# Logits beside the gate/up remainders, four units to a group, the last output in two PSUM tiles and a later output projection

## The chip, the cores and the metric

One core of a Trainium2 chip runs the whole program. The metric is the device time of one execution in microseconds (us); the kernel before took 577.35 us (median of 6 runs, 576.67 to 954.04; the highest is one run, left out of all ratios). The granted TensorE clock was 0.999 of full speed in the profiled execution.

The engines are called PE (TensorE, matmuls; PEld is its weight load), ACT (ScalarE), DVE (VectorE), POOL (GpSimd) and SP (SyncE); ACTq is ACT's queue of transfers. PSUM, in banks, is the memory that PE writes its results to.

## The reference, cut to what matters

A block with adaptive layer norm: attention over 8 dilated neighbours (32 heads of 18), then a bilinear gated MLP. There are 2048 tokens of width D = 576, and F = 4608 hidden units.

```python
h = layernorm(x) * (1 + ca) + sa
q, k, v = split(h @ wqkv)                      # 32 heads of 18
logits[s, w] = q[s] . k[s - 2 w], w = 0..7     # masked at the start
x = x + ga * (softmax(logits * scale) @ v[neighbours]) @ wo
h = layernorm(x) * (1 + cb) + sb
x = x + gb * ((h @ w_gate) * (h @ w_up)) @ w_down
```

## The kernel before: the parts that matter

The 2048 tokens go through attention in ten chunks (four of 128 tokens, six of 256). Gate/up runs in seven passes: four of 128 tokens, then three of 512. After every 512 tokens comes a "down" (four row blocks of 36 x 2 matmuls). While PE works on one pass, the attention of the next chunks is woven into its order by a pacer, a function that the kernel calls after every few matmuls: a table gives, for each piece of attention, the fraction of the period at which it is put in.

```python
AT = dict(lg0=.06, lg1=.14, lgT=.19, hT=.31, ...)                # fractions of a period
AT_FIRST = dict(AT, ..., oT=.66, wo0=.70, wo1=.74, h2T=.92)      # chunks 4 and 5 use this one
...
ps_att = pool("ps_att", 2, space=PSUM)      # 2 banks, attention
ps_mlp = pool("ps_mlp", 3, space=PSUM)      # 3 tiles of 2 banks, MLP
v_sb = once.tile([P, D], BF, name="v_sb")   # one buffer for v on its way to DRAM
```

The width of 576 is four blocks of 128 and a remainder of 64. Gate and up share the array for the remainder: gate's uses rows 0 to 63, up's rows 64 to 127, and the two matmuls run side by side in a tiling of 64 x 128. To save changes of tiling, three units (a unit is gate and up of 128 hidden columns for 512 tokens) form a group:

```python
for u in range(0, len(units), 3):
    for k in range(3):
        ps[u + k] = ps_mlp.tile([P, 2, nf, 512 // nf], F32, name="pgu", tag="mlp")
        if k < 2:
            main(u + k, True)            # 8 plain matmuls; then step(): the pacer may put in attention
    for k in range(3):
        rem(u + k, k == 2)               # 2 remainder matmuls each, 64*128 tiling
    step(6 * nf * ns / 2)
    evacuate(u); evacuate(u + 1)         # ACT copies PSUM out, DVE multiplies gate by up
    main(u + 2, False); evacuate(u + 2)
    ...                                  # cut: what follows a finished block
```

The logits of attention are also small matmuls: 20 of them in a 128 x 32 tiling, called `lgT`. A chunk has two such groups (pieces `lg0` and `lg1`).

The last row block of the whole output is done in two halves of 288 columns, so that the first half can be stored early. Both halves lie in one PSUM tile:

```python
for j in range(CM // P):
    acc = ps_mlp.tile([P, 2, 512], F32, name="acc", tag="mlp")
    halves = [[0], [1]] if r0 + (j + 1) * P == S else [[0, 1]]
    for qs in halves:
        ...                              # 36 or 72 matmuls into acc[:, q], then DVE reads acc and stores
```

In the attention of a chunk, `turn` transposes the attention output on PE into PSUM, ACT copies it to `oT` (two copies), and `wo0`, `wo1` are the output projections of the two 128-row halves. The v of a half goes from PSUM through `v_sb` (two ACT copies) to DRAM.

Of the kernel before, what the change touches and what calls it, by code (L numbers as in the profile page):

```python
# [8 lines left out]
F32 = mybir.dt.float32  # L9
# [8 lines left out]
P = 128  # L18
D = 576
DP = 640  # L20
KT = 5
# [11 lines left out]
CH = 256  # L33
# [3 lines left out]
FB = 4  # L37
AUTO = 4
GU_BUFS = 3
NB = FT // FB  # L40
# [14 lines left out]
AT = dict(lg0=.06, lg1=.14, lgT=.19, hT=.31, q0=.37, q1=.41, k0=.45, k1=.49, qkr=.52, v0=.55, v1=.58,  # L55
          ws=.60, oT=.61, wo0=.66, wo1=.70, h2T=.86)

AT_FIRST = dict(AT, hT=.24, q0=.29, q1=.34, k0=.39, k1=.44, qkr=.48, v0=.52, v1=.57, ws=.64, oT=.66, wo0=.70, wo1=.74, h2T=.92)

AT_SHORT = dict(AT_FIRST, qkr=.47, ws=.51, oT=.52, wo0=.59, v0=.66, v1=.72, h2T=.80)  # L60


@with_exitstack
def kernel(
# [13 lines left out]
    nc = tc.nc  # L78
# [7 lines left out]
    def pool(name, bufs, **kw):  # L86
        return ctx.enter_context(tc.tile_pool(name=name, bufs=bufs, **kw))
# [13 lines left out]
    ps_mlp = pool("ps_mlp", 3, space=PSUM)  # L101

    def att(shape, dt, name):
        return ps_att.tile(shape, dt, name=name, tag="att")

    def hp():
        return tc.high_priority()
# [11 lines left out]
    for sl, m0, off in ((slice(0, KT), 0, 0), (slice(KT, KT + 1), KT - 1, -64)):  # L119
        n = sl.stop - sl.start  # L120
# [15 lines left out]
    hT = once.tile([P, KT, CH], BF, name="hT")  # L136
# [5 lines left out]
    oT = once.tile([P, KT, CH], BF, name="oT")  # L142
# [7 lines left out]
    def load_x(ci, eng, js=None, behind=None):  # L150

        for j in range(SIZES[ci] // P) if js is None else js:
            xt = xin.tile([P, D], BF, name="x_t")
            if behind is not None:
                nc.vector.tensor_copy(xt[0:1, 0:1], behind)
            eng.dma_start(xt[:], x_flat[START[ci] + j * P:START[ci] + (j + 1) * P, :])
            x_tiles.setdefault(ci, []).append(xt)
# [16 lines left out]
    v0 = sp.tile([P, D], BF, name="v0")  # L174
# [83 lines left out]
    rows = {}  # L258
# [20 lines left out]
    gu_blocks = {}  # L279
# [53 lines left out]
    def block_done(pi, b):  # L333
        if pi == KEPT_PASSES - 1 and b in KEPT:
            k = KEPT.index(b)
            load_wd(k * WDB, (k + 1) * WDB)
        for n in range(len(loads)):
            if last_use[n] == (pi, b) and n + GU_BUFS == state["next"]:
                load_next(eng=nc.gpsimd if pi == 0 else nc.sync)
        if (pi, b) == (0, ORDER[0][-2]):  # L340

            for cx in (4, 5):
                load_x(cx, nc.sync, behind=late["hh"][0:1, b * FB, 0:1])
            f0 = len(KEPT) * WDB
            nc.vector.tensor_copy(wd[0:1, f0, 0:1], late["hh"][0:1, b * FB, 0:1])
            load_wd(f0, FT)
# [301 lines left out]
    def gate_up(pi, c0, C, h2, step):  # L648




        hh = late["hh"]
        cs = slice(c0, c0 + C)
        ns = C / 2.4

        def tokens(rows, kt):
            return h2[rows, :, kt, :] if C > CH else h2[rows, c0 // CH, kt, c0 % CH:c0 % CH + C]

        def by_half(ap):  # L660
            return ap.rearrange("p (a c) -> p a c", c=CH) if C > CH else ap


        nf = 2 if C <= 256 else 1
        units = [(b, i) for b in ORDER[pi] for i in range(0, FB, nf)]

        def main(u, first):
            (b, i), out = units[u], ps[u]
            for n in range(nf):
                for t in range(2):  # L670
                    for kt in range(KT - 1):
                        nc.tensor.matmul(by_half(out[:, t, n, 0:C]), lhsT=gu_blocks[b][0][:, kt, t, (i + n) * P:(i + n + 1) * P], rhs=tokens(slice(0, P), kt),  # L672
                                         start=(first and n == 0 and kt == 0), stop=(not first and kt == KT - 2), skip_group_check=True)
                step(8 * ns)

        def rem(u, first):
            (b, i), out = units[u], ps[u]
            for n in range(nf):
                for t in range(2):
                    rows = slice(64 * t, 64 * (t + 1))  # L680
                    nc.tensor.matmul(by_half(out[:, t, n, 0:C]), lhsT=gu_blocks[b][1][rows, (i + n) * P:(i + n + 1) * P], rhs=tokens(rows, KT - 1),  # L681
                                     start=(first and n == 0), stop=not first, skip_group_check=True)

        def evacuate(u):
            b, i = units[u]
            fs = slice(b * FB + i, b * FB + i + nf)
            with hp():
                g = late["gup"].tile([P, 2 * CM], BF, name="gu")[:, 0:2 * nf * C].rearrange("p (n t c) -> p n t c", n=nf, t=2)
                nc.scalar.copy(g, ps[u][:, :, :, 0:C].rearrange("p t n c -> p n t c"))  # L689
                nc.vector.tensor_tensor(hh[:, fs, cs], g[:, :, 0, :], g[:, :, 1, :], ALU.mult)  # L690


        ps, done = {}, 0
        for u in range(0, len(units), 3):
            for k in range(3):
                ps[u + k] = ps_mlp.tile([P, 2, nf, 512 // nf], F32, name="pgu", tag="mlp")
                if k < 2:
                    main(u + k, True)
            for k in range(3):
                rem(u + k, k == 2)  # L700
            step(6 * nf * ns / 2)
            evacuate(u)
            evacuate(u + 1)
            main(u + 2, False)
            evacuate(u + 2)
            while done < NB and (done + 1) * FB <= (u + 3) * nf:
                block_done(pi, ORDER[pi][done])
                done += 1

    def down(di, r0, x_t, step):  # L710
        to_load = [(cx, j) for cx in LOAD_X_DOWN.get(di, []) for j in range(SIZES[cx] // P)]
        hh = late["hh"]
        for j in range(CM // P):
            acc = ps_mlp.tile([P, 2, 512], F32, name="acc", tag="mlp")

            halves = [[0], [1]] if r0 + (j + 1) * P == S else [[0, 1]]
            for qs in halves:
                for f in range(FT):
                    for q in qs:
                        nc.tensor.matmul(acc[:, q, 0:288], lhsT=hh[:, f, j * P:(j + 1) * P], rhs=wd[:, f, q * 288:(q + 1) * 288],  # L720
                                         start=(f == 0), stop=(f == FT - 1))
                    step(120 * len(qs))
                with hp():
                    n, cs = len(qs), slice(qs[0] * 288, (qs[-1] + 1) * 288)
                    o_t = outp.tile([P, D], BF, name="y")[:, 0:n * 288]
                    nc.vector.tensor_tensor(o_t.rearrange("p (n d) -> p n d", n=n), acc[:, qs[0]:qs[-1] + 1, 0:288],  # L726
                                            gb_bc[:, cs].rearrange("p (n d) -> p n d", n=n), ALU.mult)
                    nc.vector.tensor_tensor(o_t, o_t, x_t[j][:, cs], ALU.add)  # L728
                (nc.gpsimd if n == 2 else nc.sync).dma_start(out_flat[r0 + j * P:r0 + (j + 1) * P, cs], o_t)  # L729
            if to_load:  # L730
                cx, jx = to_load.pop(0)
                load_x(cx, nc.gpsimd, [jx])

    h2T = {}
    home = {c: (di, START[c] - START[d[0][0]]) for di, d in enumerate(DOWN) for p in d for c in p}

    def attend_into_place(ci):
        di, c0 = home[ci]
        if di not in h2T:
            h2T[di] = h2p.tile([P, CM // CH, KT, CH], BF, name="h2T")  # L740
        return attend(ci, h2T[di][:, c0 // CH, :, c0 % CH:c0 % CH + SIZES[ci]])

    def period(ci):

        gens = {"a": project(ci + 1)} if ci + 1 < NCH else {}
        gens["b"] = attend_into_place(ci)
        at = AT_SHORT if SIZES[ci] == P else AT_FIRST if ci < 6 else AT
        nxt = {k: next(g) for k, g in gens.items()}
        while nxt:
# [3 lines left out]
            if nxt[k] is None:  # L753
                del nxt[k]

    class Pacer:


        def __init__(self, todo, total):
            self.todo, self.L, self.t, self.i, self.gen, self.nxt = todo, total / max(1, len(todo)), 0.0, 0, None, None  # L760

        def __call__(self, ns, rest=False):
            self.t += ns
            while self.i < len(self.todo):
                if self.gen is None:
                    if self.t < self.i * self.L and not rest:
                        return
                    self.gen = period(self.todo[self.i])
                    self.nxt = next(self.gen)
                if self.t < (self.i + self.nxt) * self.L and not rest:  # L770
                    return
                self.nxt = next(self.gen, None)
                if self.nxt is None:
                    self.gen, self.i = None, self.i + 1
                elif not rest:
                    return
# [49 lines left out]
    passes = [(di, p) for di, d in enumerate(DOWN) for p in d]  # L826
# [49 lines left out]
```

## Time and profile before

| | before |
|---|---|
| median time, us | 577.35 |
| span of the profiled execution, us | 576.4 |
| PE busy | 562.7 us (98%) |
| DVE, ACT, POOL busy | 55%, 38%, 17% |
| chain that ended last, PE's share | 84% |

The first lines of the page, busy time by engine:

```profile
PE 562.7 (98%) x5167; PEld 369.0 (64%) x5171; DVE 318.0 (55%) x695; ACT 221.5 (38%) x386; POOL 95.7 (17%) x165
```

PE is the bound, so a gain must come from time in which PE does its fixed work badly ordered, or waits. The view of waits for PE shows few waits; these three touch the change (in us: total, times, longest):

```profile
PE acc L720 <- ACT gu L689: 0.6, 1, 0.6
PE pwA L628 <- ACT oT L621: 0.6, 1, 0.6
PE acc L720 <- DVE y L726: 0.5, 1, 0.5
```

The chain that ended last, in order of time, is the best view for a bound engine: consecutive pieces add up to the span. Its columns are start, duration, and what, with the number of matmuls. First, a stretch of the first 512-token pass:

```profile
208.95 3.45 PE pgu L672 x16
212.40 0.78 PE lgT L553 x20
213.19 0.76 PE pgu L681 x6
213.94 3.56 PE pgu L672 x16
217.50 0.78 PE lgT L553 x20
218.28 1.83 PE pgu L672 x8
220.12 0.75 PE pgu L681 x6
220.87 1.83 PE pgu L672 x8
```

L672 are the plain matmuls, L681 the remainders, L553 the logits. Sixteen plain matmuls take 3.45 us (0.216 each) when they follow plain ones, but 3.56 after remainders; eight take 1.83 instead of 1.73 after remainders or after logits. Leaving a tiling mode costs 0.105 us. Six remainders are three pairs, 3 x 0.216 = 0.65, and take 0.755: entering costs 0.107. The first logits group of the chunk stands directly before remainders; the second (217.50) stands between plain matmuls and so pays an exit of its own.

The last pass, the same view: groups of 6 remainders and 24 plain matmuls, a change in and a change out every 6.04 us.

```profile
497.70 0.76 PE pgu L681 x6
498.45 5.29 PE pgu L672 x24
503.74 0.76 PE pgu L681 x6
504.49 5.29 PE pgu L672 x24
```

The end, the same view, and then the timeline of the same moment (in brackets: idle time before the instruction, and what ended it):

```profile
536.53 30.88 PE acc L720 x252
567.41 0.02 issue
567.43 0.47 DVE y L726
567.90 0.04 issue
567.95 4.58 PE acc L720 x36
```

```profile
567.43 0.46 DVE L726 TENSOR_TENSOR y<-acc,gb_bc 128x288 bf16<-128x288 f32 x1 [3.16 <-PE acc L720]
567.95 4.57 PE L720 MATMUL acc<-wd,hh 128*128 128x288 bf16 x36 [0.55 <-DVE y L726]
```

The last 36 matmuls wait for DVE to finish reading the first half, although they write another bank: both halves are one tile.

The last place is the start of the first down, chunk 4's output. The timeline of ACT there:

```profile
149.90 0.33 ACTq L517 DMA_DIRECT2D vd<-v_sb  x1
154.17 0.40 ACT L514 CAST v_sb<-pvA 128x288 bf16<-128x288 f32 x1 [2.96 <-DMA vd<-v_sb]
154.47 0.40 ACT L514 CAST v_sb<-pvB 128x288 bf16<-128x288 f32 x1
155.32 1.59 ACT L689 CAST gu<-pgu 128x512 bf16<-128x512 f32 x3 [0.45 <-PE turnA L414]
```

ACT stands still for 2.96 us until the store of v has landed and `v_sb` is free. Behind it, in order, wait the evictions of gate/up (`gu`) and then the copies to `oT`.

### The profile page before, as it was taken

What the parts mean: (1) busy time and instruction counts of PE and PEld (TensorE: products, weight loads), DVE (VectorE), ACT (ScalarE), POOL (GpSimd) and SP (SyncE); (2) the same over time, 40 slices, a digit from 0 to 9 for tenths busy, and PEclk for the clock granted to TensorE, in tenths of its full rate; (3) what the DMA queues carried; (4) which work ended last, traced back from release to release, by engine and by line L of the source; (5) the groups of instructions that cost most, each with busy time, mean ns of one, the idle gap of its engine ahead of it and who ended that gap; (6) DMA issues with size and microseconds to landing.
All of it is one profiled execution on the core that took longest, in us unless ns stands there. A gap on an engine that the chain in (4) does not pass through costs nothing.

```text
span 576.4 us, 12231 instructions
## 1 busy us (share of the span) xinstructions
PE 562.7 (98%) x5167; PEld 369.0 (64%) x5171; DVE 318.0 (55%) x695; ACT 221.5 (38%) x386; POOL 95.7 (17%) x165
## 2 busy tenths in 40 slices
PE   8898999999999999999999999999999999999996
PEld 4577898888778764554468764554457744344775
DVE  5777687868688775655494635754384422122101
ACT  3455565555502225445442005454440035454200
POOL 5552202020113212020601150011200200000000
PEclk9999999999999999999999999999999999999999
DMA  9999765259760354477302633477202224450000
GB/s 298 277 354 338 255 191 187 74 197 316 227 193 22 107 167 151 124 216 230 96 1 77 218 91 112 125 240 214 81 0 57 68 66 124 150 164 1 1 22 20
DMA packets 68457, 84.32 MB, mean 146 GB/s; under 512 B 19618, under 2 KB 59506, under 8 KB 68402
## 3 DMA queue, kind: packets, MB, share of 16 engines
q1 hardware_dynamic: 56738, 45.86, 26.8%
q0 software_dynamic: 9104, 34.44, 18.0%
q10 hardware_dynamic: 2560, 3.25, 1.7%
q8 instruction: 40, 0.66, 0.5%
q14 instruction: 15, 0.12, 0.1%
HBM read 70.93 MB, written 8.67 MB: 138 GB/s over the span
## 4 chain that ended last, share of the span: by engine, by line
PE 84%; DMA 9%; DVE 3%; ACT 2%; issue 1%; ACTq 0%; POOL 0%; DVEq 0%
PE pgu L672 40%; PE acc L720 24%; PE pgu L681 6%; PE pq L485 5%; DMA wd<-in_B_w_up_dram 4%; DMA wm<-in_w_mod_dram 4%; PE lgT L553 2%; PE pwB L628 2%; PE pwA L628 1%; DMA vd<-v_sb 1%; PE pvA L510 1%; PE pvB L510 1%; DVE ln_stats L377 1%; PE pr L492 1%; ACT gu L689 1%
## 5 line engine op out<-in xcount | busy, mean ns | idle before, releaser
L672 PE MATMUL pgu<-h2T,gm 128*128 128x512 bf16 (+1 forms) x1504 | 238.5, 311 | 1.1 <-ACT gu L689 0.7
L689 ACT CAST gu<-pgu 128x1024 bf16<-128x1024 f32 (+1 forms) x180 | 145.5, 844 | 141.7 <-PE pgu L681 115.5
L672 PEld LDWEIGHTS <-gm 128*128 128x128 bf16 x1504 | 118.4, 98 | 108.2 <-issue 16.3
L720 PE MATMUL acc<-wd,hh 128*128 128x288 bf16 x1152 | 146.5, 286 | 1.2 <-ACT gu L689 0.6
L690 DVE TENSOR_TENSOR hh<-gu 128x512 bf16<-128x512 bf16 (+1 forms) x180 | 66.2, 372 | 129.5 <-ACT gu L689 128.2
L720 PEld LDWEIGHTS <-hh 128*128 128x128 bf16 x1152 | 112.4, 98 | 30.2 <-issue 1.9
L544 DVE TENSOR_TENSOR prod<-qT,kT 128x1280 bf16<-128x1280 bf16 (+1 forms) x80 | 46.7, 633 | 14.6 <-PE lgT L553 13.4
L527 POOL DMA_DIRECT2D vsh<-vd x30 | 22.6, 757 | 155.7 <-DMA vd<-v_sb 114.7
L729 POOL DMA_DIRECT2D out_dram<-y x15 | 8.5, 563 | 214.3 <-DVE y L728 214.3
L485 PE MATMUL pq<-hT,wqk 128*128 128x256 bf16 (+1 forms) x400 | 41.2, 251 | 0.8 <-DMA wqk<-in_A_wqkv_dram 0.8
L726 DVE TENSOR_TENSOR y<-acc,gb_bc 128x576 bf16<-128x576 f32 (+1 forms) x17 | 12.2, 720 | 52.3 <-PE acc L720 52.3
L611 DVE TENSOR_TENSOR vsh<-vsh,attn 128x2304 bf16<-128x2304 bf16 x30 | 39.9, 1353 | 0.2
L681 PE MATMUL pgu<-h2T,gr 64*128 64x512 bf16 (+1 forms) x376 | 37.0, 311 | 0.0
L485 PEld LDWEIGHTS <-wqk 128*128 128x128 bf16 x400 | 32.3, 98 | 6.8 <-DMA wqk<-in_A_wqkv_dram 1.5
L672 PE MATMUL pgu<-h2T,wd 128*128 128x128 bf16 x512 | 34.9, 219 | 1.5 <-DMA wd<-in_B_w_up_dram 1.0
L672 PEld LDWEIGHTS <-wd 128*128 128x128 bf16 x512 | 30.1, 98 | 3.3 <-DMA wd<-in_B_w_up_dram 1.5
L383 ACT ACTIVATE ln_rstd<-ln_stats,eps 128x2 f32<-128x2 f32 (+1 forms) x20 | 5.9, 296 | 67.2 <-DVE ln_stats L378 67.1
L377 DVE BATCH_NORM_STATS2 ln_stats<-x_t 128x6 f32<-128x288 bf16 x64 | 26.2, 447 | 1.9 <-DMA x_t<-in_A_x_dram 1.2
L681 PEld LDWEIGHTS <-gr 64*128 64x128 bf16 x376 | 12.2, 94 | 18.9 <-issue 11.9
L425 POOL TENSOR_SCALAR h2T<-h2T,modc 128x256 bf16<-128x256 bf16 x25 | 15.7, 634 | 30.5 <-DMA h2T<-xn_d 30.5
L633 DVE TENSOR_TENSOR y<-pwA,ga_bc 128x288 bf16<-128x288 f32 x15 | 6.7, 449 | 24.6 <-PE pwA L628 24.4
L612 DVE TENSOR_TENSOR vsh<-vsh 128x2304 bf16<-128x2304 bf16 x15 | 20.3, 1353 | 0.0
(147 smaller groups left out, 454.8 us busy)
## 6 DMA issues: line engine op xcount, KB each, us to landing
vsh<-vd POOLq DMA_DIRECT2D x30, 576.0 KB, 5.9
gm<-in_B_w_gate_dram SPq DMA_DIRECT2D x24, 512.0 KB, 3.8
gm<-in_B_w_up_dram SPq DMA_DIRECT2D x24, 512.0 KB, 5.0
wd<-in_B_w_down_dram SPq DMA_DIRECT2D x4, 1152.0 KB, 8.6
gm<-in_B_w_gate_dram POOLq DMA_DIRECT2D x5, 512.0 KB, 11.9
gm<-in_B_w_up_dram POOLq DMA_DIRECT2D x5, 512.0 KB, 11.4
out_dram<-y POOLq DMA_DIRECT2D x15, 144.0 KB, 2.1
wd<-in_B_w_gate_dram POOLq DMA_DIRECT2D x4, 512.0 KB, 10.0
```

The costliest lines, as they stand in the source:

```text
L377: nc.vector.bn_stats(stats[:, j, hf, :], src[j][:, hf * 288:(hf + 1) * 288])
L485: nc.tensor.matmul(pq[:, gi, 0:C], lhsT=wqk[:, kt, w0:w0 + P], rhs=h[:, kt, :], start=(kt == 0), stop=(kt == KT - 1))
L527: nc.gpsimd.dma_start(vsh[:].rearrange("p w d h -> p w (d h)"), src)
L544: nc.vector.tensor_tensor(prod[:, 0:nm, 0:C], qT[:, 0:nm, 0:C], kT[:, 0:nm, off:off + C], ALU.mult)
L611: nc.vector.tensor_tensor(vsh[:], vsh[:], attn[:, j, ws, None, :].to_broadcast([P, WG, DH, H]), ALU.mult)
L612: nc.vector.tensor_tensor(va[:], va[:], vb[:], ALU.add)
L628: nc.tensor.matmul(pw[q][:, 0:288], lhsT=oT[:, m, j * P:(j + 1) * P], rhs=wo[:, m, q * 288:(q + 1) * 288], start=(m == 0), stop=(m == KT - 1))
L672: nc.tensor.matmul(by_half(out[:, t, n, 0:C]), lhsT=gu_blocks[b][0][:, kt, t, (i + n) * P:(i + n + 1) * P], rhs=tokens(slice(0, P), kt), s ...
L681: nc.tensor.matmul(by_half(out[:, t, n, 0:C]), lhsT=gu_blocks[b][1][rows, (i + n) * P:(i + n + 1) * P], rhs=tokens(rows, KT - 1), start=(f ...
L689: nc.scalar.copy(g, ps[u][:, :, :, 0:C].rearrange("p t n c -> p n t c"))
L690: nc.vector.tensor_tensor(hh[:, fs, cs], g[:, :, 0, :], g[:, :, 1, :], ALU.mult)
L720: nc.tensor.matmul(acc[:, q, 0:288], lhsT=hh[:, f, j * P:(j + 1) * P], rhs=wd[:, f, q * 288:(q + 1) * 288], start=(f == 0), stop=(f == FT ...
```

## The change

Four edits, none of which changes the arithmetic:

1. In 512-token passes the logits may be put in only directly before or after remainders, so that two special modes adjoin and one exit is saved.
2. In the last pass, where no attention is left, a group has four units instead of three; the fourth uses the two attention banks. Twelve groups become nine.
3. The two halves of the last output get a PSUM tile each.
4. For chunks 4 and 5 the output projection is put in a little later behind the transposes.

```diff
-AT_FIRST = dict(AT, ..., wo0=.70, wo1=.74, h2T=.92)
+AT_FIRST = dict(AT, ..., wo0=.72, wo1=.77, h2T=.92)
 ... (gate_up)
+        def psum(k):
+            if k < 3:
+                t = ps_mlp.tile([P, 2, nf, 512 // nf], F32, name="pgu", tag="mlp")
+                return [t[:, 0], t[:, 1]], t
+            return [att([P, nf, 512 // nf], F32, "pgu" + "gu"[t])[:] for t in range(2)], None
 ... (main)
-                step(8 * ns)
+                step(8 * ns, beside=beside if C > CH else None)
 ... (evacuate: one ACT copy for a tile of two banks, two for the attention banks)
+        nu = 4 if pi == len(passes) - 1 else 3
-        for u in range(0, len(units), 3):
-            for k in range(3):
+        for u in range(0, len(units), nu):
+            for k in range(nu):
 ... (the tiles of PSUM come from psum(k))
                 if k < 2:
-                    main(u + k, True)
-            for k in range(3):
-                rem(u + k, k == 2)
+                    main(u + k, True, k == 1)
+            for k in range(nu):
+                rem(u + k, k >= 2)
 ... (evacuations and the later units, for nu units instead of three)
 ... (down)
-            acc = ps_mlp.tile([P, 2, 512], F32, name="acc", tag="mlp")
             halves = [[0], [1]] if r0 + (j + 1) * P == S else [[0, 1]]
             for qs in halves:
+                acc = ps_mlp.tile([P, 2, 512], F32, name="acc", tag="mlp")
 ... (pacer)
+    BESIDE = {AT["lg0"], AT["lg1"]}
 ... (in the pacer's loop)
+                if beside is False and self.nxt in BESIDE and not rest:
+                    return
```

More of the change, by code (lines that the diff above doesn't have):

```diff
@@ L56 @@
           ws=.60, oT=.61, wo0=.66, wo1=.70, h2T=.86)
-AT_FIRST = dict(AT, hT=.24, q0=.29, q1=.34, k0=.39, k1=.44, qkr=.48, v0=.52, v1=.57, ws=.64, oT=.66, wo0=.70, wo1=.74, h2T=.92)
+AT_FIRST = dict(AT, hT=.24, q0=.29, q1=.34, k0=.39, k1=.44, qkr=.48, v0=.52, v1=.57, ws=.64, oT=.66, wo0=.72, wo1=.77, h2T=.92)
 AT_SHORT = dict(AT_FIRST, qkr=.47, ws=.51, oT=.52, wo0=.59, v0=.66, v1=.72, h2T=.80)
@@ L665, in gate_up, with main @@
         units = [(b, i) for b in ORDER[pi] for i in range(0, FB, nf)]
-        def main(u, first):
-            (b, i), out = units[u], ps[u]
+        def psum(k):
[3 more added lines that the diff above has]
+            return [att([P, nf, 512 // nf], F32, "pgu" + "gu"[t])[:] for t in range(2)], None
+        def main(u, first, beside=False):
+            (b, i), out = units[u], ps[u][0]
             for n in range(nf):
@@ L671, in main @@
                     for kt in range(KT - 1):
-                        nc.tensor.matmul(by_half(out[:, t, n, 0:C]), lhsT=gu_blocks[b][0][:, kt, t, (i + n) * P:(i + n + 1) * P], rhs=tokens(slice(0, P), kt),
+                        nc.tensor.matmul(by_half(out[t][:, n, 0:C]), lhsT=gu_blocks[b][0][:, kt, t, (i + n) * P:(i + n + 1) * P], rhs=tokens(slice(0, P), kt),
                                          start=(first and n == 0 and kt == 0), stop=(not first and kt == KT - 2), skip_group_check=True)
-                step(8 * ns)
+                step(8 * ns, beside=beside if C > CH else None)
         def rem(u, first):
-            (b, i), out = units[u], ps[u]
+            (b, i), out = units[u], ps[u][0]
             for n in range(nf):
@@ L680, in rem @@
                     rows = slice(64 * t, 64 * (t + 1))
-                    nc.tensor.matmul(by_half(out[:, t, n, 0:C]), lhsT=gu_blocks[b][1][rows, (i + n) * P:(i + n + 1) * P], rhs=tokens(rows, KT - 1),
+                    nc.tensor.matmul(by_half(out[t][:, n, 0:C]), lhsT=gu_blocks[b][1][rows, (i + n) * P:(i + n + 1) * P], rhs=tokens(rows, KT - 1),
                                      start=(first and n == 0), stop=not first, skip_group_check=True)
@@ L688, in evacuate @@
                 g = late["gup"].tile([P, 2 * CM], BF, name="gu")[:, 0:2 * nf * C].rearrange("p (n t c) -> p n t c", n=nf, t=2)
-                nc.scalar.copy(g, ps[u][:, :, :, 0:C].rearrange("p t n c -> p n t c"))
+                if ps[u][1] is not None:
+                    nc.scalar.copy(g, ps[u][1][:, :, :, 0:C].rearrange("p t n c -> p n t c"))
+                else:
+                    for t in range(2):
+                        nc.scalar.copy(g[:, :, t, :], ps[u][0][t][:, :, 0:C])
                 nc.vector.tensor_tensor(hh[:, fs, cs], g[:, :, 0, :], g[:, :, 1, :], ALU.mult)
+        nu = 4 if pi == len(passes) - 1 else 3
         ps, done = {}, 0
-        for u in range(0, len(units), 3):
-            for k in range(3):
-                ps[u + k] = ps_mlp.tile([P, 2, nf, 512 // nf], F32, name="pgu", tag="mlp")
+        for u in range(0, len(units), nu):
+            for k in range(nu):
+                ps[u + k] = psum(k)
                 if k < 2:
-                    main(u + k, True)
-            for k in range(3):
-                rem(u + k, k == 2)
-            step(6 * nf * ns / 2)
+                    main(u + k, True, k == 1)
+            for k in range(nu):
+                rem(u + k, k >= 2)
+            step(2 * nu * nf * ns / 2)
             evacuate(u)
             evacuate(u + 1)
-            main(u + 2, False)
-            evacuate(u + 2)
-            while done < NB and (done + 1) * FB <= (u + 3) * nf:
+            for k in range(2, nu):
+                main(u + k, False)
+                evacuate(u + k)
+            while done < NB and (done + 1) * FB <= (u + nu) * nf:
                 block_done(pi, ORDER[pi][done])
@@ L760, in __init__, with __call__ @@
             self.todo, self.L, self.t, self.i, self.gen, self.nxt = todo, total / max(1, len(todo)), 0.0, 0, None, None
-        def __call__(self, ns, rest=False):
+        def __call__(self, ns, rest=False, beside=None):
             self.t += ns
```

## The prediction

> **What bounds the kernel.** TensorE. The page gives PE busy 562.7 of 576.4 us (98%); the chain that ended last is 84% PE; the granted clock is 0.999. The list of waits shows only about 10 us of PE waiting. So only PE's order, mode changes and short waits can give anything, and the change touches only those.
>
> **What a mode change costs.** The Trainium skill, "TensorEngine Tiling (Array Packing)", Key Properties, says that changing the tiling mode drains TensorE. The chain in order of time agrees and gives the size: 16 plain 512-column matmuls take 3.45 us (0.216 each), but 24 after a remainder group take 5.29 instead of 5.18: 0.105 us to come out. Six remainders (three pairs of 0.216) take 0.755: 0.107 us to go in. A logits group takes 0.78 whatever follows; remainders after logits still take 0.755.
>
> **1. Logits beside remainders (512-token passes, 4 chunks).** The first logits group of each chunk already stands right before remainders; only the second (217.5, 283.6, 348.7, 414.9 us) stands between plain matmuls. By the pacing arithmetic each moves one unit later, directly before remainders, and the logits' transposes keep their place. One exit saved each: 4 x 0.105 = **0.4 us**. The ScalarE copy of the logits (0.59 us) then has 2.5 us before its reader instead of 4.3; enough.
>
> **2. Four units to a group in the last pass.** 12 groups become 9: 3 x (0.107 + 0.105) = **0.6 us**. The fourth unit uses attention banks, idle there; two ScalarE copies of an estimated 0.57 against one of 1.01. ScalarE needs about 4.2 us in a cycle of 8.0; no PE wait expected.
>
> **3. Last output in two PSUM tiles.** The timeline shows the last 36 down matmuls waiting 0.55 us (567.4 to 567.95) for VectorE's multiply of the first half. That goes: **0.5 us**.
>
> **4. wo behind the turn (chunks 4 and 5, first down).** At 157 us PE loses about 0.8 us waiting for ScalarE's copies of the turned output, at 198 us about 0.3. The first wo moves two down steps later (0.49 us), so 0.5 + 0.3 is won. But the second wo also moves, leaving 16 instead of 20 down steps (3.9 us) before the turn of chunk 5's second norm, whose norm work took 4.35 us: about 0.5 us is given back, as a wait of that turn or of the next pass's first matmul for h2T (already 0.3). Net **0.3 us**. The scheduler orders this pass, so it is the least sure.
>
> Sum 1.8 to 1.9 us, directly on PE: **575.4 us** from 577.35, range **574.0 to 577.1**. Faster by over 2%: 0.01; within 2%: 0.98; slower: 0.01.
>
> **What would show it.** All eight logits groups of the two middle 512-token passes followed by remainders; in the last pass nine groups of 8 remainders of about 0.97 us (4 x 0.216 + 0.107), each followed by 32 plain matmuls of 7.0 us, gate/up ending about 0.6 us sooner; the last 72 down matmuls without the 0.55 gap; wo's wait for the turned output shrinking from 0.56 to 0.1 to 0.3; a longer wait for the turn or h2T near the first 512-token pass. ACT about 1 us busier.
>
> **What would make it wrong.** The scheduler reordering the fourth 128-token pass, or ScalarE's queue so that an eviction precedes the logits copy and PE waits up to 1 us four times; an exit cost that differs with longer groups; the fourth unit's banks not free in time; part 4 losing more than it wins. Each is a few us at most, so 2% (11.5 us) is out of reach.

## The result, and the profile after

The changed kernel took **575.5 us** (median of 20 runs, 574.26 to 576.4) against 577.39 (median of 40 runs of the kernel before); the ratio is 0.9964, 95% interval 0.9957 to 0.9971. The ratio is the mean time of one kernel's fast runs over that of the other's of the same rounds, so it is not quite the ratio of the medians. Executions over 1.5% slower than the fastest of the same kernel are left out of the means. All results were correct.

The page and the chain, the same views as before, now with L679 for plain matmuls, L688 for remainders and L734 for down:

```profile
PE 561.8 (98%) x5167; PEld 369.9 (64%) x5171; DVE 317.8 (55%) x695; ACT 222.2 (39%) x395; POOL 93.9 (16%) x165
```

The first 512-token pass. The second logits group now stands before remainders: 24 plain matmuls in one piece ahead of it, and one exit for both modes behind.

```profile
208.23 3.45 PE pgu L679 x16
211.69 0.78 PE lgT L553 x20
212.47 0.75 PE pgu L688 x6
213.22 5.29 PE pgu L679 x24
218.51 0.78 PE lgT L553 x20
219.29 0.75 PE pgu L688 x6
220.05 1.83 PE pgu L679 x8
```

The last pass: eight remainders (six and the last pair, which has other tile names) in 0.97 us, then 32 plain matmuls in 7.01 (475.31 to 482.32).

```profile
474.34 0.76 PE pgu L688 x6
475.09 0.21 PE pgug L688
475.31 0.00 PE pguu L688
475.31 1.83 PE pgu L679 x8
477.14 0.86 PE pgug L679 x4
478.01 0.86 PE pguu L679 x4
478.87 3.45 PE pgu L679 x16
```

The end: all 288 down matmuls of the last down are one piece, without the gap.

```profile
534.75 35.29 PE acc L734 x288
570.05 0.02 issue
570.07 0.47 DVE y L740
```

Of the three waits shown before, this is left in the view of waits (by the distances between starts, wo of chunk 4 still loses 0.60 us here, 0.24 and 0.36, against 0.73 and 0.23 before):

```profile
PE pwB L628 <- ACT oT L622: 0.2, 1, 0.2
```

And ACT at the start of the first down, the store of v 0.85 us quicker in this execution:

```profile
150.29 0.33 ACTq L517 DMA_DIRECT2D vd<-v_sb  x1
153.71 0.40 ACT L514 CAST v_sb<-pvA 128x288 bf16<-128x288 f32 x1 [2.10 <-DMA vd<-v_sb]
154.01 0.40 ACT L514 CAST v_sb<-pvB 128x288 bf16<-128x288 f32 x1
154.86 1.59 ACT L697 CAST gu<-pgu 128x512 bf16<-128x512 f32 x3 [0.45 <-ACT v_sb L514]
```

The whole gain is 0.3%, while single runs of one kernel scatter by about as much. So the parts cannot be told apart by total time; but PE is never idle for long, and its stretches repeat to about 0.01 us. I cut each trace at the start times of PE's matmuls, from the first matmul of a stage to the first of the next (the last down to its modelled end, the end that the profiler gives to a matmul):

| stretch, us | before | after | difference |
|---|---|---|---|
| turn of chunk 4 to first down matmul | 1.34 | 0.67 | -0.67 |
| first down | 52.83 | 52.57 | -0.26 |
| first 512-token gate/up | 86.14 | 85.93 | -0.21 |
| second down | 45.09 | 45.09 | 0.00 |
| second 512-token gate/up | 86.14 | 85.92 | -0.22 |
| third down | 37.73 | 37.73 | 0.00 |
| last gate/up | 72.48 | 71.85 | -0.63 |
| last down | 36.15 | 35.44 | -0.71 |

These add up to -2.69. All that comes before, the set-up and the first four passes, was 0.21 longer in this execution, which leaves 2.48 of the spans' 2.5 us.

### The profile page after: what moved, and what is told of

Read it like the earlier page. It is cut to its first block, busy times and chain, and to the rows that moved or that the text cites. A ratio compares the mean times of both kernels' runs of the same rounds, so it can differ in the third digit from the quotient of the medians.

```text
span 573.9 us, 12238 instructions
## 1 busy us (share of the span) xinstructions
PE 561.8 (98%) x5167; PEld 369.9 (64%) x5171; DVE 317.8 (55%) x695; ACT 222.2 (39%) x395; POOL 93.9 (16%) x165
## 4 chain that ended last, share of the span: by engine, by line
PE 87%; DMA 8%; DVE 3%; ACT 1%; issue 1%; POOL 0%; ACTq 0%; DVEq 0%
PE pgu L679 38%; PE acc L734 24%; PE pgu L688 6%; PE pq L485 5%; DMA wd<-in_B_w_up_dram 4%; DMA wm<-in_w_mod_dram 4%; PE lgT L553 2%; PE pwB L628 1%; PE pwA L628 1%; PE pguu L679 1%; PE pgug L679 1%; PE pvA L510 1%; PE pvB L510 1%; PE warm L275 1%; DVE ln_stats L377 1%; PE pr L492 1%
## 5 line engine op out<-in xcount | busy, mean ns | idle before, releaser
L679 PE MATMUL pgu<-h2T,gm 128*128 128x512 bf16 (+1 forms) x1432 | 223.1, 308 | 1.1 <-ACT gu L697 0.7
L679 PEld LDWEIGHTS <-gm 128*128 128x128 bf16 x1504 | 119.0, 98 | 107.7 <-issue 14.2
L697 ACT CAST gu<-pgu 128x1024 bf16<-128x1024 f32 (+1 forms) x171 | 136.7, 835 | 130.0 <-PE pgu L688 103.5
L734 PE MATMUL acc<-wd,hh 128*128 128x288 bf16 x1152 | 146.4, 286 | 0.0
L734 PEld LDWEIGHTS <-hh 128*128 128x128 bf16 x1152 | 112.4, 98 | 28.8 <-issue 0.4
L679 PE MATMUL pgu<-h2T,wd 128*128 128x128 bf16 x512 | 34.9, 219 | 1.4 <-DMA wd<-in_B_w_up_dram 1.0
L688 PE MATMUL pgu<-h2T,gr 64*128 64x512 bf16 (+1 forms) x358 | 34.5, 307 | 0.0
L679 PEld LDWEIGHTS <-wd 128*128 128x128 bf16 x512 | 30.1, 98 | 3.2 <-DMA wd<-in_B_w_up_dram 1.5
L688 PEld LDWEIGHTS <-gr 64*128 64x128 bf16 x376 | 12.5, 94 | 17.5 <-issue 11.1
```

What stands on the lines that cost most here:

```text
L679: nc.tensor.matmul(by_half(out[t][:, n, 0:C]), lhsT=gu_blocks[b][0][:, kt, t, (i + n) * P:(i + n + 1) * P], rhs=tokens(slice(0, P), kt), s ...
L688: nc.tensor.matmul(by_half(out[t][:, n, 0:C]), lhsT=gu_blocks[b][1][rows, (i + n) * P:(i + n + 1) * P], rhs=tokens(rows, KT - 1), start=(f ...
L697: nc.scalar.copy(g, ps[u][1][:, :, :, 0:C].rearrange("p t n c -> p n t c"))
L734: nc.tensor.matmul(acc[:, q, 0:288], lhsT=hh[:, f, j * P:(j + 1) * P], rhs=wd[:, f, q * 288:(q + 1) * 288], start=(f == 0), stop=(f == FT ...
```

## The experiments

Twelve runs were made; e11 and e12 repeat the changed kernel and e10. All gave correct results. Three had no timing rounds (state unknown) and are read by stretches alone. The 512-token gate/up passes carry edit 1, the last gate/up edit 2 and the last down edit 3; the first two rows of the table above carry edit 4.

| run | median, us | ratio to before (95%) | turn to down | first down | 512-token gate/up | last gate/up | last down |
|---|---|---|---|---|---|---|---|
| before | 577.39 | | 1.34 | 52.83 | 86.14, 86.14 | 72.48 | 36.15 |
| after | 575.5 | 0.9964 (0.9957 to 0.9971) | 0.67 | 52.57 | 85.93, 85.92 | 71.85 | 35.44 |
| e1, logits only | 577.19 | 0.9982 (0.9967 to 0.9996) | 0.56 | 52.67 | 85.93, 85.93 | 72.48 | 36.15 |
| e2, four units only | 576.69 | 0.9977 (0.9965 to 0.9989) | 0.56 | 52.67 | 86.14, 86.14 | 71.85 | 36.15 |
| e3, output only | 577.06 | 0.9984 (0.9969 to 0.9999) | 0.56 | 52.69 | 86.14, 86.14 | 72.48 | 35.44 |
| e4, wo only | 577.35 | 0.9984 (0.9968 to 1.0) | 0.71 | 52.95 | 86.14, 86.14 | 72.48 | 36.15 |
| e5, one unit a group | 581.18, one run | | 0.82 | 52.51 | 85.92, 85.92 | 77.57 | 35.45 |
| e6, two units a group | 576.29, one run | | 0.56 | 51.91 | 85.93, 85.93 | 73.73 | 35.45 |
| e7, logits apart | 580.99, one run | | 0.56 | 52.48 | 86.35, 86.35 | 71.85 | 35.44 |
| e8, second place for v | 574.44 | 0.9954 (0.9941 to 0.9968) | 0.56 | 51.87 | 85.93, 85.93 | 71.85 | 35.44 |
| e9, e8 with wo as before | 574.82 | 0.9959 (0.9945 to 0.9974) | 0.56 | 52.03 | 85.93, 85.93 | 71.85 | 35.44 |
| e10, e8 with a nearer second wo | 574.47 | 0.9944 (0.9929 to 0.9959) | 0.56 | 51.34 | 85.93, 85.92 | 71.85 | 35.44 |
| e11, changed kernel again | 575.38 | 0.9957 (0.9942 to 0.9972) | 0.66 | 52.46 | 85.92, 85.92 | 71.85 | 35.44 |
| e12, e10 again | 574.18 | 0.9936 (0.9924 to 0.9948) | 0.56 | 51.34 | 85.92, 85.92 | 71.85 | 35.44 |

The second down is 45.09 and the third 37.73 in every run but e7.

### Each edit alone (e1 to e4)

The changed kernel with three of the four edits undone:

```diff
 # undone in e1, e2, e3
-AT_FIRST = dict(AT, ..., wo0=.72, wo1=.77, h2T=.92)
+AT_FIRST = dict(AT, ..., wo0=.70, wo1=.74, h2T=.92)
 # undone in e1, e3, e4
-        nu = 4 if pi == len(passes) - 1 else 3
+        nu = 3
 # undone in e2, e3, e4
-                step(8 * ns, beside=beside if C > CH else None)
+                step(8 * ns)
 # undone in e1, e2, e4
+            acc = ps_mlp.tile([P, 2, 512], F32, name="acc", tag="mlp")
             for qs in halves:
-                acc = ps_mlp.tile([P, 2, 512], F32, name="acc", tag="mlp")
```

> Kernel before with only the logits beside the remainders. Drain theory (each mode change costs about 0.105 us to leave): each of the two middle gate/up passes 86.14 -> 85.93 us (start of its first matmul to start of its first down matmul), everything else as before; in all 0.4 us, ratio about 0.9993. Rival (the place does not matter, the whole change's gain there came from other engines' order): no stretch changes by more than 0.05 us.

Measured: both passes 85.93, and no later stretch moved. The two stretches before them did (0.56 and 52.67 against 1.34 and 52.83), but alike in e1, e2 and e3, so not through this edit; e8 takes that up. The place of the logits is what counts; the order in which ACT, DVE and POOL do their work in e1 is that of the kernel before, so it cannot be the cause.

> Kernel before with only the four-unit groups of the last pass. Drain theory: the last gate/up pass 72.48 -> 71.84 us, three groups less of two changes of 0.106 each; ratio about 0.9989. Rival (the extra PSUM banks give slack to the evictions): also faster, but then the runs with one and two units to a group would not follow a straight line in the number of groups.

Measured: 71.85. The rest is with e5 and e6.

> Kernel before with only the last output in two PSUM tiles. The idle figure taken as it stands (0.55 us): the last down 36.15 -> 35.60 us. Rival (idle is counted from the modelled end of a matmul of 0.29 us, while matmuls start every 0.1225, so 0.165 us more was lost): 36.15 -> 35.44 us, as in the changed kernel. Ratio 0.9988 to 0.9990.

Measured: 35.44, the rival. A wait shown as 0.55 us cost 0.71. The idle figure counts from the modelled end of the matmul before (it is given 0.29 us), but the stream starts one every 0.1225 us, so the matmul after the wait starts 0.165 later against the stream than the figure says. The Trainium skill, "Perfetto Trace Analysis", section Tensor Engine Instruction, says that the profiler estimates a matmul's end from its size; this agrees, and gives the size of the error in a wait: 0.29 - 0.1225.

> Kernel before with only the later wo. The first down (its first matmul to the first of the next gate/up) 52.83 -> about 52.5 us, as in the changed kernel: about 0.65 won at the two wo's, 0.3 to 0.4 given back at the second logits of chunk 5 and at the turn of its norm. The stretch from the turn of chunk 4 to the first down matmul (1.34 us before, 0.67 after) should not depend on this edit: theory, it depends on how long the store of v took in that execution (4.2 us in the profile of before, 3.4 after), so here anything from 0.6 to 1.4. Rival: the edit moved it; then about 0.67 here and 1.34 in the other three. Ratio 0.9990 to 0.9998.

Measured: the first down came out at 52.95, not 52.5, and the stretch before it at 0.71. e1, e2 and e3, without the edit, have 0.56 there, so the edit did not shorten that stretch: the 1.34 in the profile of before was a matter of that one execution. What moves it, and the first down's shortfall (0.48 us lost before the turn of chunk 5), is taken up in e8. By totals, all four intervals hold the expected ratio, but they are too wide to rank the parts, and the four shortfalls add up to 0.0073, twice that of the whole change (the runs of before in that call had a median of 577.94 us, 0.55 above that of all 40, so all four ratios look too good): totals alone would have misled here.

### How much a change of mode costs (e5, e6, e7)

```diff
 e5: -nu = 4 if pi == len(passes) - 1 else 3
     +nu = 1 if pi == len(passes) - 1 else 3     (and evacuate(u + 1) only if nu > 1)
 e6: +nu = 2 if pi == len(passes) - 1 else 3
 e7: -main(u + k, True, k == 1)
     +main(u + k, True, k == 0)
     -step(2 * nu * nf * ns / 2)
     +step(2 * nu * nf * ns / 2, beside=False if C > CH else None)
```

> Changed kernel, but one unit to a group in the last pass: 36 groups, and each group has one pair of remainders. PSUM as in the kernel before. Drain theory, a cost per change of mode: a straight line through 12 groups (72.48) and 9 (71.85), 0.21 us a group, so 77.5 us for the last gate/up. Rival (slack of the fourth unit's banks): about 72.5, since three tiles serve it as before.

> Changed kernel, but two units to a group in the last pass: 18 groups. Drain theory: 73.74 us for the last gate/up. Rival (slack of banks): about 72.5.

Measured: 77.57 with 36 groups, 73.73 with 18, 72.48 with 12, 71.85 with 9. That is 0.213 us a group from 18 to 36, 0.208 from 12 to 18 and 0.21 from 9 to 12: a straight line. Slack of PSUM has no part in it, for one, two and three units use the same three tiles. So a cost per change of mode is shown. That it is a drain, the array emptying, is not shown apart from a rival: the single instructions in the trace of before show that in the plain stream a weight load (PEld) starts about 2 ns after the start of the matmul ahead of its own, so almost a whole matmul early, while at the change to remainders at 226.31 us the first load starts only 307 ns after the start of the last plain matmul and its matmul 4 ns after the load (on the way out, at 227.06 us, 304 and 5 ns). How much of the 0.105 us is emptying and how much a weight load (92 to 96 ns) that could not run ahead, no run separates. The chain of e5 shows one group every 2.15 us, the pair of remainders at 0.32 = 0.216 + 0.107:

```profile
466.68 0.32 PE pgu L688 x2
467.00 1.83 PE pgu L679 x8
468.83 0.32 PE pgu L688 x2
```

> Changed kernel, but every logits group of the two middle gate/up passes set between plain matmuls (four in each pass; before it was two, in the changed kernel none). Drain theory: 85.93 + 4 x 0.105 = 86.35 us in each of the two passes. Rival (place does not matter): 85.93.

Measured: 86.35 in both passes, as the drain theory has it: 85.93, 86.14 and 86.35 for none, two and four logits groups standing alone. Something else happened in e7 that I had not expected: the third down took 42.06 us instead of 37.73. The later logits delayed the whole chain of chunk 9's attention, and its transposing DMA landed too late for wo:

```profile
PE pwA L628 <- DMA oT<-o_d: 2.5, 1, 2.5
```

PE's starts are 2.77 us apart there, 2.65 more than in the stream. The rest of the 4.33 us lost is the clock: from 0.4 us after the wait the matmuls start every 0.240 us instead of 0.1225, thirteen of them, until 3.7 us after the wait. The view by stretches (columns: stretch and its length; PE, PEld, DVE, ACT and POOL busy, each with the number of instructions; granted clock; DMA share and GB/s) shows it:

```profile
444.00:448.00 4.00, 1.84 (x10) 1.24 (x11) 0.00 (x0) 0.00 (x0) 0.00 (x0) 0.82 0.37 72
448.00:452.00 4.00, 4.00 (x26) 2.86 (x25) 3.34 (x8) 0.00 (x0) 0.57 (x1) 0.75 0.05 18
```

That the delay came from the logits, and not from a slow transfer alone, shows in the start times: counted from the first matmul of the third down, the second logits group comes at -5.33 us in e7 and -9.54 in the changed kernel, and the last piece of the attention output (`o_sb`) at 13.50 and 9.53.

So the place of the logits is not free to choose by mode changes alone: the changed kernel moved each of four groups by one unit and nothing broke; e7 moved all eight, by up to a group, and one wait cost 4.3 us, forty times a mode change's 0.105.

### What made the first down vary (e8)

```diff
-                vt = v0 if ci == 0 else v_sb
+                vt = v0[:] if ci == 0 else xn[:, 0, 0:D] if j else v_sb[:]
 ... (the copies and the store take vt as it is)
```

`xn`, the normalised input of the chunk, has been transposed by then and is dead until the next chunk. So the second half of v gets a place of its own and ACT need not wait for the first half's store.

> Changed kernel with a second place for v (the second 128 rows of a chunk's v go through the first rows of the normalised input, which are dead by then), so that ScalarE's copies of v need not wait for the store of the rows before. Theory (the store's time is what moved the turn-to-down stretch between 0.56 and 1.34 us, and the 20 down matmuls before chunk 5's turn by 0.1 to 0.5): 0.56 us in every execution, no extra in the 20 down matmuls, the first down at about 52.4. Total 0 to 0.6 us better than the changed kernel, ratio to before about 0.9955 to 0.9965. Rival (the stretch varies for another reason): the waits stay.

Measured: 0.56 and 51.87, even better than expected, and the wait is gone from the trace:

```profile
151.82 0.40 ACT L514 CAST xn<-pvA 128x288 bf16<-128x288 f32 x1 [0.53 <-PE pvA L510]
153.51 1.80 ACT L697 CAST gu<-pgu 128x512 bf16<-128x512 f32 x3 [0.98 <-PE pgu L688]
```

Against the changed kernel's 52.57, wo of chunk 4 won its whole 0.60 and the turn of chunk 5 its 0.10. To see why, I read from every trace the time from the issue of that store to the ACT copy that follows it, and the time PE lost from the turn of chunk 4 to the end of its second wo, beyond its matmuls at full pace:

| run | wo | store to copy, us | PE time lost at chunk 4, us |
|---|---|---|---|
| e3, e1, e2, before | old place | 3.15, 3.23, 3.23, 4.27 | 0.81, 0.89, 0.88, 1.75 |
| e6, e7, e11, after, e4, e5 | new place | 2.74, 3.08, 3.40, 3.42, 3.46, 3.56 | 0.03, 0.36, 0.69, 0.71, 0.74, 0.86 |
| e9 | old place, second place for v | 1.84 | 0.24 |
| e8, e10, e12 | new place, second place for v | 1.83 to 1.84 | 0.00 |

With wo at the new place, the loss is the store's time less 2.7 us, nearly to the hundredth, in six different executions. The path is ACT's queue: copy of v (waits for the store), evictions of gate/up, copies to `oT`, and PE waits for the last of these. The Trainium skill, "TensorE: Matmul & The Clock Gate", in its table of engine data, calls ScalarE's queue strictly first in, first out; this agrees: in the profile of before, the last three evictions began at 155.32 us, although the remainders that finish the first of them started at 153.09, and in e8 the eviction began 0.33 us after its remainders started (153.51 and 153.18).

The same table tells what the later wo won at chunk 4: at a store time of 3.23 us the old place lost 0.88 to 0.89 and the new one would have lost about 0.51 (an estimate on its line), so 0.37 us. At chunk 5 it won 0.29 (its wo took 1.51 before and 1.23 after), but only 0.21 against e1 and e2, where chunk 5's own store was quick (1.98 and 1.91 us to the copy; 3.61 in before).

Chunk 5's store has a second effect, which explains e4. The 20 down matmuls before the turn of chunk 5 take 2.45 us in most runs, but 2.93, 2.69 and 2.55 in e4, e7 and after, where the store of v of chunk 5 took 4.13, 3.88 and 3.74 us to the copy; in e5, at 3.67, they take 2.48. That is the store's time less 3.64 us. In e4 it cost 0.48 us, and without it the first down would be 52.47, as expected (52.5).

### What the later wo gave back (e9, e10)

```diff
 e9:  e8 with wo0=.70, wo1=.74
 e10: e8 with (cut: the line that picks AT_4 for chunk 4 and AT_5 for chunk 5)
 +AT_4 = dict(AT_FIRST, wo0=.72, wo1=.755)             # chunk 4
 +AT_5 = dict(AT_FIRST, wo0=.72, wo1=.755, lg1=.15)    # chunk 5
```

> The run with the second place for v, with wo back at its old place. Theory: most of what the later wo won at chunk 4 was time lost to the late store of v, so without that wait the old place costs only 0.29 us at chunk 5, and the 0.30 us given back at the second logits of chunk 5 (1.15 to 1.02) and at the turn of its norm (0.72 to 0.56) comes home: first down 51.87 -> about 51.86 us, same total. Rival (the wait of wo at chunk 4 is there without the store too): wo's 0.6 to 0.7 us come back there, first down about 52.4.

Measured: 52.03, between the two theories and nearer the first. The second logits group came back from 1.15 to 1.02 us and the turn of chunk 5's norm from 0.72 to 0.56, as expected; chunk 5's wo lost 0.21. But wo at chunk 4 lost 0.24 even without the store's wait, which I had put at nothing: there two matmuls start at 156.09 us, and the next only at 156.58, when the second copy to `oT` (155.92, 0.60 us) is done. So of the 0.9 us lost there before, about 0.65 was the store.

> The run with the second place for v, with the second wo only 10 instead of 12 down steps after the turn's place in the order (the first stays at the new place), and chunk 5's second logits one down step later. Theory: the later first wo keeps its gain and the give-back goes: turn of chunk 5's norm 0.72 -> about 0.56 us, second logits 1.15 -> about 0.8; first down 51.87 -> about 51.35 us, total about 0.5 us better than with the second place alone; ratio to before about 0.995. Rival (the give-back does not hang on the second wo): 51.87 as it was.

Measured: 51.34 against 51.35 expected; the second logits took 0.79 and the turn 0.56. So the 0.16 us at the turn of the norm hang on the second wo: VectorE starts the norm of the second half only after it, and the turn stands behind the norm. For the second logits it is not shown: e10 also put them one down step later, and they won 0.36 us, more than the 0.14 that the later wo had cost them.

### The changed kernel and the best one on the same chip (e11, e12)

e11 is the changed kernel as it is, e12 is e10 once more.

> The changed kernel once more, beside the next one on the same chip. Theory: all stretches after the first down repeat to 0.02 us; the turn-to-down stretch falls anywhere from 0.56 to 1.34 and the first down from 52.4 to 53.0 us, with the time of the store of v. Ratio to before about 0.9964. Rival: the profile of the changed kernel was typical and the stretch comes out at 0.67 again.

> The run with the second place for v and the nearer second wo, once more, on the same chip as the changed kernel. Theory: turn to down 0.56 and first down 51.34 us again, 0.5 to 1.3 us less than the changed kernel; ratio to before about 0.9945 to 0.9955, that is 0.001 to 0.002 below the changed kernel's.

Measured: 575.38 us (574.58 to 576.54) and 574.18 us (573.86 to 574.29). The ranges do not overlap, and the ratios to before, 0.9957 and 0.9936, differ by 0.0021, just above the 0.001 to 0.002 that was expected (0.9936 itself lies below the expected 0.9945 to 0.9955). e12's stretches repeat e10's to 0.01 us; e11's turn-to-down stretch repeated at 0.66, because the store took 3.40 us again (3.42 in the first profile), so that run did not tell the theory from its rival; the table above does. e12 is the version that beats both kernels, by some 3.2 us against before.

## Why the prediction was right, point by point

The prediction was 575.4 us within 574.0 to 577.1; measured were 575.5 and, again, 575.38. The step-by-step sum:

| step | predicted | measured | by |
|---|---|---|---|
| 1. logits beside remainders | 0.4 | 0.42 | e1: 2 x 0.21; e7 by the same cost |
| 2. four units | 0.6 | 0.63 | e2; slope of e5 and e6 |
| 3. last output in two tiles | 0.5 | 0.71 | e3 |
| 4. wo behind the turn, net | 0.3 | about 0.28 to 0.36, an estimate: 0.37 + 0.21 (or 0.29) - 0.30 | first down, for equal times of the stores |
| sum | 1.8 to 1.9 | about 2.1 | ratio 0.9964 of 577.39: 2.08 |

**What bounds the kernel** was right: edits 1 to 3 showed up in the stretches where they lie, in full. Edit 4 did not by itself: in e4 the first down was longer than before (52.95 against 52.83), and its gain is read only after the stores' times are taken out. Without the wait for the store of chunk 4 at all, it is 0.16 us (e9 against e8).

**The cost of a change of mode** (0.105 out, 0.107 in) was right, and e5 to e7 show that it does not depend on group length or on which special mode stands there. Why a change costs this is not settled here (see e6). The Trainium skill, "TensorEngine Tiling (Array Packing)", section Key Properties, says only that changing the mode drains the engine; the number comes from this trace.

**Step 3 was under-sized.** The term "0.55 us" was the idle figure taken as it stands; the loss was 0.71, because idle is counted from a modelled end. In step 4 I had compared starts with the stream's pace and so got 0.8 where the list of waits has 0.56.

**Step 4 was right in its sum, with two terms off.** The gain at chunk 4 was about 0.37, not 0.5, at equal store time, and that at chunk 5 0.21 to 0.29, for 0.3. The give-back was 0.30, not 0.5, and not where I put it: 0.16 at the turn of the norm, 0.14 at the second logits group of chunk 5, nothing at the next pass's first matmul. There I misread the list of waits: its 0.3 us for h2T is in both kernels, but not at that place; the first 512-token gate/up follows its down matmuls without a gap. And I did not see that the loss at 157 us was mostly set by the store of v, which differs from execution to execution. The profiled execution of before had the slowest store of all, so its profile shows a loss there that is not typical, and the two profiles differ by 2.5 us where the runs differ by about 2. That the number came within 0.1 us is partly luck: the measured steps add up to 0.2 us more than was forecast, and the interval of the ratio alone spans 0.8 us.

**Rivals.** Reordering of other engines' queues: there was some in the first down, from edit 4 alone, and none that PE waited for in edits 1 to 3. The fourth unit's banks were free in time. ACT was 0.7 us busier, for the extra copies, off the critical path.

What stays open: how the cost of a mode change divides between emptying the array and the weight load behind it, and why the store of v takes 2.7 to 4.3 us from issue to the copy that waits for it. With no wait in the way, the store's time to landing does not matter, so it was not followed up.

## What to carry to other kernels

On a bound PE, count the changes of tiling mode in its order and put special modes side by side: here 0.21 us for each pair of changes saved, a straight line over 9 to 36 groups. Measure lost PE time by start-to-start distances, not by the idle figure, and compare stretches between stage starts when the total gain is smaller than the scatter of runs. A single-buffered tile on its way to DRAM can hold up unrelated evictions behind it in an in-order queue; before tuning the place of a waiting consumer, look at what the queue ahead of its producer waits for.

## What the Trainium skill lacked or had wrong

- "TensorEngine Tiling (Array Packing)", Key Properties: no cost for the drain. Here 0.105 us to leave and 0.107 us to enter a tiling of 64 x 128, and 0.105 to leave 128 x 32; going from 128 x 32 straight to 64 x 128 costs no more than entering from plain matmuls.
- "TensorE: Matmul & The Clock Gate", section Back-to-back issue gap, gives a sustained 131 ns per matmul of 512 columns and 81 ns at 128 columns for a stream of weight load and matmul pairs. Here each matmul has its weight load, and the distances are 216 ns and 56 ns (and 122.5 at 288 columns): the page's own formula for the isolated gap, N / 2.4 + 2.5 ns, fits all three, the sustained figures neither.
- The same page, Part 1, tells of the clock falling to half after an idle window of about 3.4 us. In e7 a shorter wait was enough: 2.5 us of idle PE, with PE at work for 0.9 us of the 3.4 us before the fall, was followed by a granted clock of 0.50 (446.6 to 449.9 us) and 13 matmuls at half pace within 4 us of the wait's end, which made a wait of 2.65 us cost 4.3.
- "Perfetto Trace Analysis", section Tensor Engine Instruction, says that the end of a matmul is estimated, but not what follows for waits: an idle figure after a stream of 288-column matmuls is 0.165 us too small (0.55 shown, 0.71 lost).
